# Agent attention and a max-out feed-forward layer in one kernel: the hand-written order of instructions replaced by another, and the last output tiles scaled by one engine instead of two

## The chip, the cores and the metric

The kernel runs on one core of a Trainium2 chip. The metric is the device time of one execution in microseconds (us), smaller being better. The times below are of three executions.

## The reference

Two layers run one after the other. The first is attention through 49 "agents" for each of 4 batches of 12544 rows of 128 numbers; the second is a feed-forward layer on all 50176 rows with three input matrices of 128 x 768, whose products are combined by a maximum.

```python
def sm(a, b):
    s = scale * (a @ b.transpose(0, 2, 1))
    s = s - s.max(-1, keepdims=True)
    e = np.exp(s)
    return e / (e.sum(-1, keepdims=True) + 1e-09)
a2k = sm(agents, k)
agent_v = a2k @ v
q2a = sm(q, agents)
x = (q2a @ agent_v)                       # rows of all batches, one after the other
h = np.maximum(np.maximum(x @ w1, x @ w2), x @ w3)
out = h @ w_out
```

## The kernel before

The kernel folds the two layers into each other. For a batch b it first goes over all keys and values: it computes the exponentials of agents times keys, their sums, and the values that they weight. That gives a 49-row matrix, the agent values. Their products with the feed-forward matrices (the differences w3 - w1 and w2 - w1, and w1 times w_out) are kept as a tile `G` of 49 rows, used for all queries of that batch. A query tile then needs only its exponentials `e`, two products with `G` (`u` and `v`), two maxima, and the product with `w_out`.

**Names.** Every step is a small function with a name, made in `graph()` and put out by the class `Emit`. `kl`, `vl` and `ql` are loads of keys, values and queries; `kc`, `vc` and `qc` are their casts to bf16; `kt`, `ke`, `ks`, `kx` are the turn of a key chunk, its copy out of PSUM, its scores and its exponentials; `to` and `kv` add the sums and the weighted values into one PSUM tile `acc`. `vd` is the part of a value cast that VectorE does. A chunk is nine tiles of 128 rows; the first batch has ten such chunks and two of four tiles (numbers 10 and 11). `wm.0` to `wm.9` are ten spare products with the identity, whose results nobody reads.

**The head.** Of the first batch everything has to be loaded before any query can be finished. When the last value chunk is in, the step `rc0` sums the columns of `acc` and takes the reciprocal (lines 434 and 436), and `nr0` scales the agent values (L439). `gpa`, `gpc`, `gpb`, `gpd` are the products with the differences (L450), `gva` to `gvd` their copies into `G` (L457 on ScalarE, L459 on VectorE). The differences themselves are `d31a`, `d31b`, `d32`, `d21a`, `d21b` on VectorE (L409); `cw1`, `tw1`, `ew1`, `pl`, `el` prepare w1 times w_out.

**The body.** There are 49 query blocks s of 1024 rows. Each has scores and exponentials (`sc`, `ex`), the sums and their reciprocals (`su` L556, `re` L561), six pairs of products `u.s.f` and `v.s.f` (L569) with a first maximum on ScalarE (`a`, L582), a second on VectorE (`x`, L585), and two output tiles of 128 x 512 with the products `li` and `p` (L606, L615) and the scaling `ov` on VectorE (L624). The chunks of the next batch's keys and values are worked off between the products of the blocks. The last block, number 48, has one output tile of four row tiles and two of two (`o.48.1`, `o.48.2`). The last of these lies in a two-bank PSUM buffer, one row tile in each bank: its first row tile is scaled by VectorE (`ov.48.2`), the other by ScalarE (`ow.48`, L631). The four parts of the block are stored one by one (`st.48.0` to `st.48.3`, L639), the last from ScalarE's queue.

**What sets the order.** Nothing is scheduled by a machine. A long text, `ORDER`, names all 2901 steps in the order in which they are issued; each engine works its own steps in that order. A number behind a slash is the buffer that the step's new tile takes from its class (`SLOTS`): there are 13 load buffers, 3 for bf16 keys, 4 for bf16 values, 3 two-bank PSUM buffers (`UV`) and 2 one-bank ones (`OM`). A step that reuses a buffer waits for the last reader of the tile before it. All loads, the turns by DMA and nearly all stores are issued by SyncE, also in that order.

Of the kernel before, what the change touches and what calls it, by code (L numbers as in the profile page):

```python
# [115 lines left out]
def graph(plan, em):  # L116
# [93 lines left out]
    for s in range(NQ):  # L210
# [61 lines left out]
class Emit:  # L272
# [315 lines left out]
    def out_chunks(self, s, o):  # L588

        if s < NQ - 1 or o == 0:  # L590
            return [(4 * o + i, i * C) for i in range(4)]
        return [(4, 0), (5, C)] if o == 1 else [(6, 0), (7, 512)]

    def out_linear(self, s, o):
        def fn():
            of = [p[0] for p in parts_of(s) for _ in range(p[4])]
            out, chunks = self.flat(f"o.{s}.{o}") if o == 2 else self.t[f"o.{s}.{o}"], self.out_chunks(s, o)
            if o == 2:
                for j, c in chunks:
                    jj, h = j // 2, j % 2  # L600
                    self.nc.tensor.matmul(out[:, c:c + C], self.t[f"e.{s}"][:, jj * P:(jj + 1) * P],
                                          self.t[f"G{of[jj]}"][:, C1O + h * C:C1O + (h + 1) * C], start=True, stop=False, skip_group_check=True)
                return
            for j, c in chunks[::2]:
                jj = j // 2
                self.nc.tensor.matmul(out[:, c:c + 2 * C], self.t[f"e.{s}"][:, jj * P:(jj + 1) * P],  # L606
                                      self.t[f"G{of[jj]}"][:, C1O:C1O + 2 * C], start=(c == 0), stop=False, skip_group_check=True)
        return fn

    def out_hidden(self, s, o, f):  # L610
        def fn():
            out = self.flat(f"o.{s}.{o}") if o == 2 else self.t[f"o.{s}.{o}"]
            for j, c in self.out_chunks(s, o):
                jj, h = j // 2, j % 2
                self.nc.tensor.matmul(out[:, c:c + C], self.t[f"r.{s}.{f}"][:, h, jj * P:(jj + 1) * P], self.wo_bf[:, f, :],  # L615
# [3 lines left out]
    def out_scale(self, s, o):  # L619
        def fn():  # L620
            chunks = self.out_chunks(s, o)
            j, n = chunks[0][0], 1 if o == 2 else len(chunks)
            out = self.flat(f"o.{s}.{o}") if o == 2 else self.t[f"o.{s}.{o}"]
            self.nc.vector.tensor_tensor(out=self.t[f"os.{s}"][:, j:j + n, :],  # L624
                                         in0=out[:, :n * C].rearrange("p (j c) -> p j c", c=C),
                                         in1=self.t[f"rc.{s}"][:, j:j + n].unsqueeze(2).to_broadcast([P, n, C]), op=ALU.mult)
        return fn

    def out_scale_last(self, s):
        def fn():  # L630
            self.nc.scalar.activation(self.t[f"os.{s}"][:, 7, :], self.flat(f"o.{s}.2")[:, 512:512 + C], AF.Copy,  # L631
                                      scale=self.t[f"rc.{s}"][:, 7:8])
        return fn
# [48 lines left out]
kl0.10/0 kc0.10/0 kl0.5/1 kl0.0/2 kc0.5/1 prep kc0.0/2 kt0.0/0 kt0.10/1 kt0.5/2 ke0.10/0 ke0.0/1 vl0.7/3 kl0.7/4 kl0.6/5 vc0.7/0  # L682
kc0.7/2 kc0.6/1 kt0.6/0 ke0.6/2 ks0.0/1 kt0.7/0 ke0.7/1 ks0.7/0 ke0.5/1 kx0.0/0 ks0.6/1 ks0.5/2 kl0.11/6 vl0.5/7 kl0.1/8 kc0.11/0
kx0.5/1 to0.0/0 kt0.11/2 ke0.11/1 vc0.5/1 kx0.6/2 ql.0/9 kl0.9/0 kc0.9/2 kt0.9/2 to0.5 kv0.5 kx0.7/3 to0.7 ks0.11/0 kx0.11/1
kl0.2/1 vl0.0/2 kc0.2/1 vc0.0/1 kv0.0 kv0.7 vl0.2/3 qc.0/0 vl0.11/4 qt.0/1 ke0.9/2 ks0.9/0 kx0.9/3 vc0.2/0 qe.0/0 vc0.11/1 vd0.11
ks0.10/2 vl0.10/10 kl0.8/6 kl0.4/5 vl0.9/11 to0.6 wm.1/1 kc0.1/0 kt0.1/1 kt0.2/0 ke0.1/0 to0.9 ke0.2/2 wm.0/1 ks0.2/0 vl0.6/12
sc.0/1 kc0.4/0 kt0.4/1 vc0.9/2 kv0.9 to0.11 kv0.11 kx0.10/0 to0.10 ex.0/0 kc0.8/1 kt0.8/2 ke0.4/2 ke0.8/1 kl0.3/0 vl0.8/7 kx0.2/3
# [5 lines left out]
pl/1 el u.0.4/1 a.0.4 sc.1/0 kc1.2/2 v.0.0/2 x.0.0/2 gl/1 gvl ex.1/1 v.0.3/0 x.0.3/3 v.0.4 x.0.4/4 qt.2/1 qe.2/0 u.1.5/2 a.1.5/0  # L693
li.0.0/0 p.0.0.0 u.0.2/1 a.0.2/2 vc1.0/0 v.1.5/0 x.1.5/5 u.1.2/2 a.1.2/1 vl1.2/2 p.0.0.4 p.0.0.5 v.0.2/1 x.0.2/6 u.1.3/0 a.1.3/0
sc.2/1 ex.2/2 p.0.0.3 p.0.0.1 v.1.3/2 x.1.3/7 u.1.4/1 a.1.4 u.1.1/0 a.1.1/2 p.0.0.2 ov.0.0/0 li.0.1/1 p.0.1.2 p.0.1.4 v.1.2/2
v.1.4 x.1.4/4 x.1.2/6 p.0.1.1 p.0.1.5 u.2.5/0 a.2.5/0 p.0.1.3 p.0.1.0 ov.0.1 u.2.4/1 a.2.4 v.1.1/2 x.1.1/2 ql.4/3 qc.3/1 qt.3/0
qe.3/0 u.1.0/0 a.1.0/1 li.1.0/1 v.2.4 x.2.4/3 v.1.0/2 x.1.0/1 p.1.0.2 p.1.0.3 kt1.0/2 p.1.0.1 ks1.0/0 su.1 v.2.5/0 x.2.5/0 kx1.0/3
# [205 lines left out]
```

## Time and profile before

| what | value |
|---|---|
| times of three executions | 446.63, 445.02, 448.14 us |
| median | 446.63 us |
| the profiled execution | 447.16 us |
| its span, first to last instruction | 445.4 us |
| so outside the span | 1.76 us |
| mean granted TensorE clock | 0.996 |
| TensorE, VectorE, ScalarE, GpSimd busy | 423.2, 390.5, 393.1, 169.5 us |

The profile is of one execution, and its times are microseconds from the start of the span. PE is TensorE's matmul stream and PEld its weight loads, DVE is VectorE, ACT is ScalarE, POOL is GpSimd, SP is SyncE. In the timeline a row gives the start, the duration, the engine, the line of the kernel, the operation, the tile written and the tiles read, and in brackets how long the engine had been idle and what ended that. PE rows join several matmuls, and their ends are modelled.

### The profile page before, as it was taken

The numbers are of one execution on the slowest core, as the hardware profiler recorded it, in microseconds if no ns is written. First come the engines' busy times: TensorE is split into PE (matmuls) and PEld (weight loads), VectorE is DVE, ScalarE is ACT, GpSimd is POOL, SyncE is SP. The second block draws the span as 40 slices with busy tenths as digits, with TensorE's granted clock in tenths as the row PEclk, the third lists the DMA queues.
The fourth block names the chain that finished last, engine by engine and source line by source line (L and its number), as shares of the span: only waits on it lengthen the run. The fifth ranks groups of instructions, "written<-read, shape, count | busy, mean of one in ns | idle before, by whom it ended". The sixth has DMA issues, their size and how long they took to land.

```text
span 445.4 us, 12837 instructions
## 1 busy us (share of the span) xinstructions
PE 423.2 (95%) x5247; PEld 270.6 (61%) x5247; DVE 390.5 (88%) x495; ACT 393.1 (88%) x462; POOL 169.5 (38%) x176
## 2 busy tenths in 40 slices
PE   2687999999999999999999999999999999999996
PEld 2464466666666666666666666665665655556676
DVE  2335898999999999999999899999999999999996
ACT  2258899999998999999999999999999999999983
POOL 3522645468537437380745435354402002000000
PEclk9999899999999999999999999999999999999999
DMA  8999999999999999999999999999997952562144
GB/s 322 410 411 349 349 297 233 296 411 313 274 415 308 237 385 352 328 202 360 415 410 202 247 331 307 284 295 308 250 252 220 232 164 71 120 198 64 49 168 166
DMA packets 99158, 122.50 MB, mean 275 GB/s; under 512 B 72536, under 2 KB 75292, under 8 KB 99100
## 3 DMA queue, kind: packets, MB, share of 16 engines
q1 hardware_dynamic: 98752, 121.46, 90.9%
q8 instruction: 41, 0.67, 0.6%
q10 hardware_dynamic: 347, 0.23, 0.2%
q14 instruction: 18, 0.14, 0.1%
HBM read 78.74 MB, written 25.69 MB: 234 GB/s over the span
## 4 chain that ended last, share of the span: by engine, by line
PE 86%; DMA 4%; ACT 4%; DVE 3%; issue 2%; SPq 0%; POOL 0%; DVEq 0%; ACTq 0%; POOLq 0%
PE UV L569 35%; PE OM L615 31%; PE OM L606 6%; PE OM L544 3%; PE OM L387 3%; DMA LD<-in_k_dram 2%; PE OM L534 2%; PE OM L370 2%; ACT AS L582 2%; DMA LD<-in_v_dram 2%; DVE R L585 2%; PE OM L556 1%; PE UV L353 1%; ACT VB L344 1%; DVE OS L624 1%
## 5 line engine op out<-in xcount | busy, mean ns | idle before, releaser
L585 DVE TENSOR_TENSOR R<-UV,AS 128x1024 bf16<-128x1024 f32 x245 | 293.0, 1218 | 17.4 <-PE UV L569 14.3
L582 ACT ACTIVATE AS<-UV 128x1024 bf16<-128x1024 f32 x245 | 246.2, 1025 | 18.0 <-PE UV L569 13.8
L569 PE MATMUL UV<-EQ,G 49*128 49x512 bf16 (+1 forms) x1248 | 183.1, 370 | 0.8 <-ACT AS L582 0.2
L615 PE MATMUL OM<-wo_bf,R 128*128 128x128 bf16 x2340 | 178.7, 220 | 0.0
L615 PEld LDWEIGHTS <-R 128*128 128x128 bf16 x2352 | 139.1, 98 | 42.1 <-issue 39.6
L569 PEld LDWEIGHTS <-G 49*128 49x128 bf16 x1248 | 60.9, 93 | 62.8 <-issue 22.6
L528 POOL CAST QB<-LD 128x1024 bf16<-128x1024 f32 x49 | 50.9, 1043 | 109.7 <-DMA LD<-in_q_dram 59.2
L624 DVE TENSOR_TENSOR OS<-OM,RC 128x512 f32<-128x512 f32 x98 | 66.9, 683 | 3.4 <-PE OM L615 2.3
L346 POOL CAST KB<-LD 128x1152 bf16<-128x1152 f32 (+2 forms) x45 | 50.0, 1118 | 35.6 <-DMA LD<-in_k_dram 24.7
L576 ACT ACTIVATE UV<-UV 128x1024 f32<-128x1024 f32 x49 | 49.8, 1017 | 2.7 <-PE UV L569 1.6
L579 ACT ACTIVATE R<-UV 128x1024 bf16<-128x1024 f32 x49 | 50.2, 1024 | 1.1 <-PE UV L569 0.4
L346 POOL CAST VB<-LD 128x1152 bf16<-128x1152 f32 (+1 forms) x33 | 37.2, 1137 | 34.2 <-DMA LD<-in_v_dram 22.6
L485 POOL TENSOR_TENSOR EA<-EA,EK 128x441 f32<-128x441 f32 x27 | 27.6, 1024 | 31.2 <-ACT EK L376 31.0
L606 PE MATMUL OM<-G,EQ 128*128 128x256 bf16 x195 | 37.8, 275 | 0.0
L550 ACT ACTIVATE EQ<-OM 128x512 bf16<-128x512 f32 x49 | 29.5, 603 | 1.4 <-PE OM L544 1.4
L358 DVE COPY KT<-UV 128x1152 bf16<-128x1152 bf16 (+1 forms) x12 | 8.3, 702 | 18.3 <-PE UV L353 17.7
L606 PEld LDWEIGHTS <-EQ 128*128 128x128 bf16 x195 | 12.3, 97 | 15.0 <-issue 14.7
L370 PEld LDWEIGHTS <-KT 128*128 128x128 bf16 x392 | 15.0, 100 | 8.5 <-DVE KT L358 4.1
L544 PE MATMUL OM<-QT,agT 128*64 128x512 bf16 (+1 forms) x104 | 19.9, 388 | 0.0
L387 PE MATMUL OM<-EK,VB 128*128 128x49 bf16 x392 | 17.6, 187 | 2.2 <-ACT VB L344 1.5
L376 ACT ACTIVATE EK<-OM 128x441 bf16<-128x441 f32 (+1 forms) x33 | 18.0, 544 | 1.1 <-PE OM L556 0.5
L387 PEld LDWEIGHTS <-VB 128*128 128x128 bf16 x392 | 14.4, 98 | 7.4 <-issue 4.0
(73 smaller groups left out, 191.4 us busy)
## 6 DMA issues: line engine op xcount, KB each, us to landing
LD<-in_q_dram SPq DMA_DIRECT2D x48, 512.0 KB, 7.4
out_dram<-OS SPq DMA_DIRECT2D x48, 512.0 KB, 5.3
LD<-in_k_dram SPq DMA_DIRECT2D x40, 576.0 KB, 9.6
LD<-in_v_dram SPq DMA_DIRECT2D x40, 576.0 KB, 8.8
LD<-in_k_dram SPq DMA_DIRECT2D x3, 512.0 KB, 6.9
LD<-in_v_dram SPq DMA_DIRECT2D x3, 512.0 KB, 7.4
LD<-in_moe_w_dram SPq DMA_DIRECT2D x6, 192.0 KB, 8.2
KT<-KB SPq DMA_TRANSPOSE x33, 5.7
```

The lines of the kernel that those rows point to most:

```text
L346: (self.nc.gpsimd if eng == POOL else self.nc.vector).tensor_copy(out=out, in_=src)
L387: self.nc.tensor.matmul(out, vb[:, j, :], e[:, j * A:(j + 1) * A], start=False, stop=True, skip_group_check=True)
L528: return lambda: self.nc.gpsimd.tensor_copy(out=self.t[f"qb.{s}"], in_=self.t[f"q.{s}"][:, :GT, :])
L544: self.nc.tensor.matmul(self.t[f"qs.{s}"][h * H:(h + 1) * H, jj * P:(jj + pairs) * P], self.agT[:, b, :], self.t[f"qT.{s}"][:, 2 * jj + h: ...
L569: self.nc.tensor.matmul(t[:, h, jj * P:(jj + pairs) * P], self.t[f"G{b}"][h * H:h * H + A, c + f * P:c + (f + 1) * P], self.t[f"e.{s}"][h ...
L576: return lambda: self.nc.scalar.activation(self.t[f"u.{s}.{f}"], self.t[f"u.{s}.{f}"], AF.Relu)
L579: return lambda: self.nc.scalar.activation(self.t[f"r.{s}.{f}"], self.t[f"u.{s}.{f}"], AF.Relu)
L582: return lambda: self.nc.scalar.activation(self.t[f"a.{s}.{f}"], self.t[f"u.{s}.{f}"], AF.Relu)
L585: return lambda: self.nc.vector.tensor_tensor(out=self.t[f"r.{s}.{f}"], in0=self.t[f"v.{s}.{f}"], in1=self.t[f"a.{s}.{f}"], op=ALU.max)
L606: self.nc.tensor.matmul(out[:, c:c + 2 * C], self.t[f"e.{s}"][:, jj * P:(jj + 1) * P], self.t[f"G{of[jj]}"][:, C1O:C1O + 2 * C], start=(c ...
L615: self.nc.tensor.matmul(out[:, c:c + C], self.t[f"r.{s}.{f}"][:, h, jj * P:(jj + 1) * P], self.wo_bf[:, f, :], start=False, stop=True, ski ...
L624: self.nc.vector.tensor_tensor(out=self.t[f"os.{s}"][:, j:j + n, :], in0=out[:, :n * C].rearrange("p (j c) -> p j c", c=C), in1=self.t[f"r ...
```

## The change

`ORDER` is replaced by another text. The same steps are in it, without `ow.48`. From the first line on the loads come in another sequence (the set of nineteen loads up to `vl0.9` is the same, and so is the sequence of the six value and key loads and the six weight loads behind it), the key chunks are turned in another order, the ten spare products stand elsewhere, and buffers are numbered anew. Between the blocks 1 and 31 steps of GpSimd and SyncE, single products `p` and the order of neighbouring `u`, `v`, `a`, `x` differ; from the second output tile of block 31 on the order of the steps is the same up to the buffers' numbers. In the last block both `o.48.1` and `o.48.2` now lie as 256 adjacent columns in one bank, `li.48.2` is one product of 256 columns where it was two of 128, and `ov.48.2` scales both row tiles on VectorE in one instruction; `ow.48` and its function are gone.

```diff
-            add(f"ov.{s}.{o}", DVE, em.out_scale(s, o), (0.19, 0.28) if o == 2 else (0.345, 0.45) if quarter else (0.634, 0.72),
+            add(f"ov.{s}.{o}", DVE, em.out_scale(s, o), (0.345, 0.45) if quarter else (0.634, 0.72),
                 after=[f"p.{s}.{o}.{f}" for f in range(NF)] + [f"re.{s}"],
...
-            if o == 2:
-                add(f"ow.{s}", ACT, em.out_scale_last(s), (0.28, 0.37), after=[f"p.{s}.{o}.{f}" for f in range(NF)] + [f"re.{s}"],
-                    use=[f"o.{s}.{o}", f"rc.{s}", f"os.{s}"])
...
     def out_chunks(self, s, o):
-        if s < NQ - 1 or o == 0:
-            return [(4 * o + i, i * C) for i in range(4)]
-        return [(4, 0), (5, C)] if o == 1 else [(6, 0), (7, 512)]
+        return range(4) if o == 0 else range(4, 8) if s < NQ - 1 else range(2 * o + 2, 2 * o + 4)

     def out_linear(self, s, o):
...
+            out, tiles = self.flat(f"o.{s}.{o}"), self.out_chunks(s, o)
+            for j in tiles[::2]:
+                c = (j - tiles[0]) * C
+                self.nc.tensor.matmul(out[:, c:c + 2 * C], self.t[f"e.{s}"][:, j // 2 * P:(j // 2 + 1) * P],
+                                      self.t[f"G{of[j // 2]}"][:, C1O:C1O + 2 * C], start=(c == 0), stop=False, skip_group_check=True)
...
-    def out_scale_last(self, s):
-        def fn():
-            self.nc.scalar.activation(self.t[f"os.{s}"][:, 7, :], self.flat(f"o.{s}.2")[:, 512:512 + C], AF.Copy,
-                                      scale=self.t[f"rc.{s}"][:, 7:8])
-        return fn
```

The order from the cast of value chunk 9 to the first products of block 0, before and after:

```diff
-vc0.9/2 kv0.9 to0.11 kv0.11 kx0.10/0 to0.10 ex.0/0 kc0.8/1 kt0.8/2 ke0.4/2 ke0.8/1 kl0.3/0 vl0.8/7 kx0.2/3
-to0.2 vc0.10/1 vc0.6/2 ks0.1/0 ks0.8/2 kv0.2 kx0.8/1 vl0.4/8 vl0.3/9 wm.5/1 kv0.6 wm.6/1 ks0.4/2 kx0.1/3 to0.1 vl0.1/1 lw3a/2
-lw1a/3 lw1b lw2a/11 lw3b lw2b kc0.3/1 kt0.3/0 ke0.3/2 wm.2/1 ql.1/0 qc.1/0 ks0.3/0 vd0.10 kv0.10 lwo/10 cwo vc0.8/2 ql.2/7 qc.2/1
-kx0.4/2 to0.4 vc0.4/0 wm.8/2 kx0.3/0 to0.3 ql.3/8 kl1.1/12 to0.8 kv0.4 wm.7/0 wm.4/2 vl1.0/6 kl1.0/5 kl1.2/4 vc0.3/1 kv0.3 kv0.8
-rc0/0 d31a vc0.1/0 kv0.1 nr0/0 cw1 su.0/1 re.0/0 wm.3/2 gpa/0 gva wm.9/2 d21a gpc/1 gvc u.0.1/0 a.0.1/0 d31b d32 gpb/2 tw1/1 d21b
-gpd/1 kc1.1/1 kc1.0/0 gvb u.0.5/2 a.0.5/1 gvd v.0.1/0 x.0.1/0 u.0.3/1 a.0.3/2 ew1 qt.1/0 qe.1/0 u.0.0/2 a.0.0/0 v.0.5/0 x.0.5/1
+to0.6 ke0.9/2 kt0.11/0 ke0.11/0 ks0.11/0 kx0.11/2 vc0.0/0 vd0.11 to0.11 kv0.11 ke0.1/0 ks0.1/2 kx0.1/2 kt0.4/0 kl0.3/7 vl0.8/8
+ke0.2/0 vl0.4/6 ks0.10/2 kv0.0 to0.1 vc0.9/0 ks0.9/1 kx0.9/0 kc0.8/2 ke0.4/1 kt0.8/0 vc0.6/1 vl0.3/10 sc.0/1 ke0.8/2 ks0.8/0
+wm.2/1 to0.9 kv0.5 kv0.9 vl0.1/2 vc0.10/2 ks0.2/1 kx0.2/0 kx0.8/1 lw3a/9 lw1a/3 kv0.6 lw1b lw2a/12 lw3b lw2b ex.0/0 ks0.4/1
+kc0.3/2 kt0.3/0 to0.8 ql.1/7 qc.1/0 lwo/0 cwo kx0.4/3 to0.4 to0.2 kv0.2 vc0.8/1 kx0.10/0 vc0.4/3 ke0.3/1 ks0.3/0 to0.10 kv0.8
+wm.9/2 wm.6/1 kx0.3/1 to0.3 wm.1/0 su.0/1 re.0/0 wm.7/1 ql.2/6 qc.2/1 vd0.10 kv0.4 wm.4/1 rc0/0 vc0.3/1 d31a wm.3/0 vl1.0/5 kv0.3
+kv0.10 vc0.1/0 kv0.1 cw1 wm.8/0 nr0/0 gpa/0 gva wm.5/1 kl1.0/2 d21a kc1.0/2 gpc/2 gvc kl1.1/10 u.0.1/0 a.0.1/0 d31b d32 gpb/1 d21b
+gpd/2 gvb u.0.5/1 a.0.5/1 gvd vc1.0/0 v.0.1/0 x.0.1/0 u.0.3/2 a.0.3/2 tw1/0 ew1 qt.1/1 qe.1/0 u.0.0/1 a.0.0/0 kl1.2/8 kc1.1/1
```

The last steps, before and after:

```diff
-ov.48.1 st.48.2 p.48.2.4 p.48.2.0 p.48.2.5 p.48.2.1 p.48.2.3 ow.48 ov.48.2 st.48.3
+ov.48.1 st.48.2 p.48.2.4 p.48.2.0 p.48.2.5 p.48.2.1 p.48.2.3 ov.48.2 st.48.3
```

More of the change, by code (lines that the diff above doesn't have):

```diff
@@ L681 @@
 ORDER = """
[L682 to L685, printed above, removed]
@@ L694 @@
[L694 to L697, printed above, removed]
@@ L870 @@
-p.48.0.0 x.48.4/12 p.48.0.4 x.48.3/7 p.48.0.3 li.48.1/1 ov.48.0/2 li.48.2/0 p.48.1.5 st.48.1 st.48.0 p.48.1.2 p.48.2.2 p.48.1.1
-p.48.1.0 p.48.1.4 p.48.1.3 ov.48.1 st.48.2 p.48.2.4 p.48.2.0 p.48.2.5 p.48.2.1 p.48.2.3 ow.48 ov.48.2 st.48.3
+kl0.10/0 kc0.10/0 kl0.5/1 kl0.0/2 kc0.5/1 prep kt0.10/0 kt0.5/1 kc0.0/0 kt0.0/2 ke0.0/0 ke0.10/1 kl0.7/3 vl0.7/4 vc0.7/0 kl0.6/5
+kc0.6/0 kt0.6/0 ke0.6/2 kl0.1/6 kc0.7/1 kt0.7/2 ks0.0/0 ke0.7/0 ks0.7/2 kx0.0/0 ke0.5/0 ks0.5/1 to0.0/0 ks0.6/0 kx0.5/1 ql.0/7
+kl0.9/8 vl0.11/9 wm.0/1 vc0.11/1 kx0.7/2 to0.7 kx0.6/3 kl0.11/0 kc0.11/1 qc.0/0 qt.0/1 kc0.9/0 kt0.9/0 to0.5 vl0.2/1 kl0.2/2
```

382 lines of the change are left out of this document (187 added, 195 removed).

## The prediction

> **What bounds the kernel now.** I read the page first, for the shape of the whole.
>
> ```profile
> PE 423.2 (95%) x5247; PEld 270.6 (61%) x5247; DVE 390.5 (88%) x495; ACT 393.1 (88%) x462; POOL 169.5 (38%) x176
> ...
> PE   2687999999999999999999999999999999999996
> ...
> DMA  8999999999999999999999999999997952562144
> ```
>
> There is a head of some four slices (11 us each) in which TensorE is not full and the DMA engines are, and then a body in which TensorE never rests. Then I cut the span into windows; the columns are the window, its length, the busy time of PE, PEld, DVE, ACT and POOL, the granted clock, the DMA share and GB/s.
>
> ```profile
> 28.00:30.00 2.00, 1.94 (x20) 1.92 (x19) 0.76 (x1) 1.31 (x3) 0.68 (x1) 1.00 1.03 415
> ...
> 37.40:40.80 3.40, 2.56 (x46) 1.63 (x47) 0.56 (x2) 3.40 (x5) 0.00 (x0) 1.00 0.87 304
> 40.80:44.20 3.40, 2.21 (x23) 0.95 (x23) 3.37 (x10) 2.25 (x4) 1.17 (x1) 0.99 1.01 347
> 44.20:47.60 3.40, 3.40 (x22) 1.60 (x21) 2.14 (x4) 1.53 (x3) 1.90 (x2) 0.51 1.00 385
> ...
> 48.00:335.00 287.00, 286.38 (x3642) 182.33 (x3641) 271.12 (x341) 272.65 (x323) 142.94 (x145) 1.00 1.07 309
> 335.00:442.00 107.00, 106.68 (x1243) 66.94 (x1239) 101.44 (x112) 97.15 (x108) 9.25 (x9) 1.00 0.50 144
> ```
>
> From 48 to 442 us TensorE lacks 0.94 us of 394, with VectorE and ScalarE at some 94%. So the body moves as a whole: what the head gives or loses comes out at the end, as long as the pace of the body stays. The head ends when the agent values are scaled (L439), and just behind it the clock is at 0.51 for 3.4 us. Four places can move: the end of the loads' work, the short chain behind it, the clock, and the last stores.
>
> **The loads and ScalarE.** The timeline of ScalarE from the last wait for a load:
>
> ```profile
> 29.74 1.16 ACT L344 ACTIVATE VB<-LD 128x1152 bf16<-128x1152 f32 x1 [0.69 <-DMA LD<-in_v_dram]
> 30.81 0.32 ACT L376 ACTIVATE EK<-UV 128x196 bf16<-128x196 f32 x1
> 31.79 0.60 ACT L550 ACTIVATE EQ<-OM 128x512 bf16<-128x512 f32 x1 [0.66 <-PE OM L544]
> ...
> 38.03 0.55 ACT L376 ACTIVATE EK<-UV 128x441 bf16<-128x441 f32 x1
> 38.44 2.23 ACT L344 ACTIVATE VB<-LD 128x1152 bf16<-128x1152 f32 x2
> ```
>
> The same casts by form (shortest, middle and longest ns):
>
> ```profile
> L344 ACT ACTIVATE VB<-LD x12: 406/1159/1183, 9.2 to 39.5; 128x1152 bf16<-128x1152 f32 x10, 128x256 bf16<-128x256 f32 x2
> ```
>
> At 29.74 it starts the cast `vc0.9`, whose load it waited for, so it had no backlog then. From there it does thirteen more steps up to the end of `vc0.1` at 38.44 + 2.23 = 40.67, with one wait of 0.66 us, for `sc.0` on TensorE. In the new order the loads ahead of `vl0.9` are the same nineteen, so it should land at the same time; behind `vc0.9` there are again one small and five full value casts, `ex.0`, five full exponentials and a small one, only in another sequence (`kx0.9` instead of `kx0.1`). So `vc0.1` can end at 40.67 - 0.66 = 40.0 at the earliest. What can be late instead is `kx0.2`: TensorE's queue ahead of it holds `kt0.8`, `sc.0`, `ks0.8`, a spare product, `to0.9`, `kv0.5`, `kv0.9`, `ks0.2`, which is 9 transposes, 36 small products and 3 long ones.
>
> ```profile
> 24.90 0.93 PE L387 MATMUL OM<-EK,VB 128*128 128x49 bf16 x18 [1.54 <-ACT VB L344]
> 27.05 0.54 PE L381 MATMUL OM<-EK,ones_bf 128*128 128x441 bf16 x1
> 28.08 2.08 PE L353 MATMUL UV<-ident,KB 128*128 128x128 bf16 x18
> 32.69 0.66 PE L353 MATMUL UV<-ident,KB 128*128 128x128 bf16 x9
> 33.27 0.35 PE L381 MATMUL OM<-EK,ones_bf 128*128 128x441 bf16 x1
> 39.68 0.64 PE L387 MATMUL OM<-EK,VB 128*128 128x49 bf16 x18
> ```
>
> The upper three rows are slow and the lower three fast, though the clock column says 1.00 for 28 to 30 us: the durations show that TensorE only came to speed near 31 us. By the slow rows the queue takes 9 x 2.08/18 + 36 x 0.93/18 + 3 x 0.54 = 4.5 us, by the fast ones 0.66 + 36 x 0.64/18 + 3 x 0.35 = 3.0. It starts with the cast of key chunk 8, whose load is the one ahead of `vl0.9`. That is 0.59 MB at 415 GB/s, or 1.4 us earlier, near 28.3; with a cast on GpSimd (1.17 in the row of `qc.1` further down) TensorE can start at 29.5. `kx0.2` may then start between 32.5 and 34.0, while ScalarE comes to it at 29.74 + 1.16 + 0.55 + 1.16 + 0.41 = 33.0 (`vc0.9`, `kx0.9`, `vc0.6`, and the small `vc0.10`, of whose form the line L344 has 0.406). So the new wait is between 0 and 1.0 us. I take 0.36, because the clock rose near 31 us, a third into this queue: -0.66 + 0.36 = **-0.3 us**, bounds -0.66 and +0.4.
>
> **From the last cast to the agent values.** The chain goes through VectorE:
>
> ```profile
> 40.36 0.62 DVE L434 TENSOR_REDUCE KR<-OM 128x49 f32<-128x441 f32 x1 [2.84 <-PE OM L387]
> 41.01 0.46 DVE L436 RECIPROCAL KR<-KR 128x49 f32<-128x49 f32 x1
> 41.39 0.49 DVE L409 TENSOR_TENSOR wall<-LD,LD 128x384 bf16<-128x384 f32 x1
> 41.80 0.20 DVE L439 TENSOR_TENSOR avT<-OM,KR 128x49 bf16<-128x49 f32 x1
> 41.91 0.20 DVE L561 RECIPROCAL RC<-OM 128x8 f32<-128x8 f32 x1
> 42.03 2.42 DVE L409 TENSOR_TENSOR wall<-LD,LD 128x384 bf16<-128x384 f32 x5
> ```
>
> ```profile
> 41.03 0.39 PE L387 MATMUL OM<-EK,VB 128*128 128x49 bf16 x9 [0.71 <-DVE KR L434]
> ```
>
> Today `rc0` stands behind `kv0.3` and `kv0.8`, and `kv0.1` waits 0.71 us until the reduction has read `acc`; then `d31a` stands ahead of the scaling. From the end of `vc0.1` to the scaling are 41.80 - 40.67 = 1.13 us. In the new order `rc0` follows `kv0.4`, which hangs on `vc0.4`, a cast that ended before `kx0.3`; so reduction, reciprocal and `d31a` (40.36 to 41.88, 1.5 us) run while ScalarE does the last two casts (2.23 us). `rc0` itself starts some 1.3 us after `kx0.3`: `to0.3`, `su.0`, `kv0.4` and two spares stand ahead of it, each of some 0.3. `d31a` then ends 2.8 us after `kx0.3`, the last values at 2.23 + 0.39 + 0.05 = 2.7. So the scaling starts some 0.65 to 0.75 us after `vc0.1`, instead of 1.13: **-0.4 us**, bounds -0.55 and 0, the latter if `rc0` is held up. Behind the scaling `re.0` (41.91 to 42.03, 0.12) no longer stands ahead of `d21a`: **-0.1 us**.
>
> **The differences beside GpSimd.** `gpb` at 44.03 waits for `d31b` and `d32`, three pieces of 128 columns.
>
> ```profile
> L409 DVE TENSOR_TENSOR wall<-LD,LD x6: 283/499/1123, 41.4 to 43.9; 128x384 bf16<-128x384 f32 x3, 128x128 bf16<-128x128 f32 x3
> ```
>
> ```profile
> 42.67 1.17 POOL L528 CAST QB<-LD 128x1024 bf16<-128x1024 f32 x1 [8.04 <-DMA LD<-in_q_dram]
> 44.03 0.50 PE L450 MATMUL UV<-wall,avT 128*64 128x384 bf16 x2 [0.65 <-DVE wall L409]
> 44.47 0.82 PE L421 MATMUL OM<-ident,w_bf 128*128 128x128 bf16 x6
> 45.22 0.53 PE L450 MATMUL UV<-wall,avT 128*64 128x384 bf16 x2
> 45.68 1.46 PE L569 MATMUL UV<-EQ,G 49*128 49x512 bf16 x6
> ```
>
> One piece took 1.123 us where another took 0.283, while GpSimd cast `qc.1` from 42.67 to 43.84. The Trainium skill, GPSIMD Engine Reference, section 1 (Specifications), says that GpSimd's SBUF interfaces are shared with VectorE and that instructions with two SBUF inputs contend; the row agrees with it. If all comes some 0.8 us earlier and `qc.1` does not (its load stands behind the same bytes), the pieces are through before the cast and 1.123 - 0.283 = 0.84 us goes; if `qc.1` comes earlier too, nothing. I take **-0.3 us**, bounds -0.84 and 0.
>
> **The clock and `tw1`.** Between 44.2 and 47.6 us TensorE ran at 0.51, which costs up to 3.4 x 0.49 = 1.67 us of its work. The window before that has 2.21 us of TensorE in 3.4. In the new order six spare products stand between `kx0.3` and `gpc` where there were four (0.35 each), and the wait of 0.71 goes, so the stretch is denser; `tw1` (0.82) leaves the place between `gpb` and `gpd`, so `u.0.5` can follow `gvb`, at up to 0.5 us less. What the clock gives is not won whole, since u, a, v, x pass through three engines. How busy the window must be the trace doesn't say; 2.56 in 3.4 was enough before it. Half a chance of about 0.8 is **-0.4 us**, bounds -1.67 and +1.7 (a second slow window). The Trainium skill, TensorE: Matmul & The Clock Gate, Part 1, says that the clock falls after an idle window of about 3.4 us; here it fell without a gap of even 1 us, so the measurement decides against that wording, and by that rule neither kernel would lose here.
>
> **The tail.**
>
> ```profile
> 441.30 0.72 PE L615 MATMUL UV<-wo_bf,R 128*128 128x128 bf16 x10
> 441.50 0.42 DVE L624 TENSOR_TENSOR OS<-OM,RC 128x256 f32<-128x256 f32 x1 [0.31 <-PE OM L615]
> 442.06 0.37 ACT L631 ACTIVATE OS<-UV,RC 128x128 f32<-128x128 f32 x1 [2.44 <-PE UV L615]
> 442.46 0.29 DVE L624 TENSOR_TENSOR OS<-UV,RC 128x128 f32<-128x128 f32 x1 [0.53 <-ACT OS L631]
> 442.79 0.38 ACTq L639 DMA_DIRECT2D out_dram<-OS  x1
> ```
>
> The two halves are not scaled at once: VectorE waits for ScalarE. From 442.06 to 442.75 are 0.69 us; one piece of 256 columns has a row of its own, 0.42. So **-0.27 us**, firm within 0.1. The product `li.48.2` in one piece stands on a queue that still waits for others: 0.
>
> **The body.** The steps moved between blocks 1 and 31 are the same steps, and no duration changes. Their cover is the 0.94 us slack of TensorE and the waits of VectorE for products:
>
> ```profile
> DVE R L585 <- PE UV L569: 10.9, 32, 0.8
> ```
>
> These are 10.9 us in 32 waits from 44 to 335 us. I take 0, bounds -1 and, if the cover is gone, one more such amount.
>
> **The sum:** -0.3 - 0.4 - 0.1 - 0.3 - 0.4 - 0.27 = -1.77 us. Against the profiled execution, 447.16 us, that is 445.39; that execution is 0.53 above the median of the three runs, so for a median run I say 446.63 - 1.77 = **444.9 us**.
>
> **The rivals.**
>
> *The wait moves.* TensorE is still slow at the queue ahead of `kx0.2`, so ScalarE waits 1.0 us and `vc0.1` ends at 41.0. With +0.4, -0.4, -0.1, the cold window as before and the tail -0.27, the time is 446.63 - 0.37 = 446.3. For it speaks the slow rate up to 31 us; against it that the new order has TensorE dense from the cast of chunk 4 on.
>
> *A second slow clock window* (slower): the value chunks come in 1.15 us steps and TensorE has 0.4 us of work for each, so the clock can fall before the products and again stay low behind them. The head's -0.3 - 0.4 - 0.1 and the tail's -0.27 stay, and +1.67 comes: 447.2. Against it: 2.56 of 3.4 us held the clock.
>
> *The body loses its pace* (slower): with the products in another order between blocks 1 and 31, VectorE waits longer for v. It has 94% to do, so it cannot catch up. From a total of 10.9 + 1.8 = 12.7 us of such waits on, the change is a loss; at three quarters more, +8.2, the time is 446.63 - 1.77 + 8.2 = 453.1. For it: three engines are nearly full, and nothing in the trace bounds it. Against it: in each block u, a, v, x keep nearly their sequence.
>
> *The head gives all.* The wait for `sc.0` goes whole (0.66), the chain gives 0.55 and 0.12, the contention 0.84, the clock stays up (1.67), `u.0.5` follows `gvb` (0.5), the tail 0.27: -4.6, 442.0 us.
>
> **How the numbers follow.** The forecast, 443.4 to 446 with 444.9 in it, has 0.45; the moved wait 0.19, the second slow window 0.13, the body 0.13, the full gain 0.10. The range of 442.8 to 449.0 us takes in the forecast, the first two rivals and the spread of the runs (445.02 to 448.14), and leaves out most of the last two. About 1% (4.5 us) is what a measurement of this kernel can tell from no change. Faster by more than that is under 442.2, half of the full gain: 0.05. Slower by more is over 451.1, nearly all of the body's rival: 0.12. The rest, 0.83, is within.
>
> **What would show it.** In the new profile: the scaling L439 starts at 40.6 to 41.3 instead of 41.80; L434 runs before the last value cast ends, and the last L387 no longer waits for it; no wait for L544 on ScalarE, or another one for L370 of at most 1.0; the longest L409 piece is under 0.5; the clock from 43 to 48 us is above 0.51; the last L624 is one of 128x256 with 0.42, followed by the store. DVE's waits for UV between 44 and 335 us stay near 10.9. The forecast is wrong if L439 is later than 41.8, if the clock is low for over 4 us, or if TensorE's busy time from 48 to 335 us falls under 285.

## The result, and the profile after

| | before | after |
|---|---|---|
| median of 12 runs, us | 446.19 (443.56 to 450.42) | 443.01 (442.27 to 444.06) |
| ratio after / before | | 0.9927 [0.9901, 0.9953] |
| profiled execution, us | 447.16 (span 445.4) | 442.68 (span 440.9) |

The new kernel is 3.2 us faster at the median. Its runs lie within 1.8 us, those of the old one within 6.9. The forecast was 444.9 in a range of 442.8 to 449.0; the measured time lies 0.2 us above the low end of that range and below the 443.4 to 446 that had the largest chance. The ratios here and below leave out executions more than 1.5% above the fastest of their kernel, so they are not the quotients of the medians beside them. The code lost three lines above the places of the head, so L439 is now L436, L409 is L406, L450 is L447, L569 is L566 and L585 is L582; further down it lost more, and L624 is now L611.

First the windows of the new profile, with the same edges as before (window, length, busy time of PE, PEld, DVE, ACT and POOL, granted clock, DMA share, GB/s):

```profile
37.40:40.80 3.40, 2.99 (x42) 1.39 (x37) 3.18 (x10) 2.91 (x6) 0.00 (x0) 1.00 1.08 370
40.80:44.20 3.40, 3.02 (x29) 1.50 (x30) 3.09 (x6) 3.00 (x5) 1.87 (x2) 1.00 1.05 395
44.20:47.60 3.40, 3.29 (x29) 1.68 (x30) 3.40 (x4) 3.40 (x6) 1.37 (x2) 1.00 1.02 406
48.00:335.00 287.00, 286.30 (x3653) 182.53 (x3650) 271.06 (x340) 271.42 (x320) 143.96 (x147) 1.00 1.10 312
```

The clock stays at 1.00 and the body keeps its pace: 286.30 of 287 us against 286.38. So the time came from the head and the tail. Rows of the new timeline of ScalarE up to its last value cast:

```profile
18.28 0.54 ACT L373 ACTIVATE EK<-UV 128x441 bf16<-128x441 f32 x1 [2.27 <-PE UV L367]
...
25.69 0.33 ACT L373 ACTIVATE EK<-UV 128x196 bf16<-128x196 f32 x1 [2.18 <-PE UV L367]
...
28.35 1.17 ACT L341 ACTIVATE VB<-LD 128x1152 bf16<-128x1152 f32 x1 [0.84 <-DMA LD<-in_v_dram]
...
31.27 0.42 ACT L341 ACTIVATE VB<-LD 128x256 bf16<-128x256 f32 x1 [0.28 <-PE OM L384]
...
36.30 2.23 ACT L341 ACTIVATE VB<-LD 128x1152 bf16<-128x1152 f32 x2
```

`vc0.1` ends at 36.30 + 2.23 = 38.53 instead of 40.67. VectorE and TensorE behind it:

```profile
38.66 0.49 DVE L406 TENSOR_TENSOR wall<-LD,LD 128x384 bf16<-128x384 f32 x1
39.07 0.20 DVE L436 TENSOR_TENSOR avT<-OM,KR 128x49 bf16<-128x49 f32 x1
39.34 1.78 DVE L406 TENSOR_TENSOR wall<-LD,LD 128x384 bf16<-128x384 f32 x5
40.70 0.82 PE L447 MATMUL UV<-wall,avT 128*64 128x384 bf16 x4
41.72 0.85 PE L566 MATMUL UV<-EQ,G 49*128 49x512 bf16 x6 [0.19 <-DVE G L456]
42.43 1.23 DVE L582 TENSOR_TENSOR R<-UV,AS 128x1024 bf16<-128x1024 f32 x1 [0.31 <-PE UV L566]
```

The row of before for that last one, `x.0.1`, the first result of block 0:

```profile
46.83 1.23 DVE L585 TENSOR_TENSOR R<-UV,AS 128x1024 bf16<-128x1024 f32 x1 [0.48 <-PE UV L569]
```

Read as a chain, the 4.40 us between the two profiles at `x.0.1` are:

| step | before | after | difference |
|---|---|---|---|
| end of `vc0.1` | 40.67 | 38.53 | -2.14 |
| `vc0.1` to the scaling `nr0` | 1.13 | 0.54 | -0.59 |
| `nr0` to `gpb` | 2.23 | 1.63 | -0.60 |
| `gpb` to `u.0.5` | 1.65 | 1.02 | -0.63 |
| `u.0.5` to `x.0.1` | 1.15 | 0.71 | -0.44 |

The last two lie nearly whole in the window whose clock was 0.51 before (from 44.2). At the end:

```profile
437.08 0.72 PE L604 MATMUL UV<-wo_bf,R 128*128 128x128 bf16 x10
437.84 0.42 DVE L611 TENSOR_TENSOR OS<-UV,RC 128x256 f32<-128x256 f32 x1
438.29 0.39 ACTq L620 DMA_DIRECT2D out_dram<-OS  x1
```

From the end of the last product to the issue of the store are 438.29 - 437.80 = 0.49 us; before they were 442.79 - 442.02 = 0.77. The span ends 3.1 us after the last product (440.9 - 437.80), and ended 3.4 after it before (445.4 - 442.02), so the end comes earlier by as much.

A caution on reading one pair of profiles: the old kernel's executions differ among themselves. Each run has the mean clock that was granted, and one window of 3.4 us at half clock lowers it by about 0.004 (3.4 x 0.5 of some 443 us). So a change's own effect is read here from the runs at full clock, and the clock is counted apart. Full clock means a mean of 0.999 or more, and a window at half clock is called cold. Beside the experiments the old kernel ran at full clock in 17 of 35, 21 of 35 and 11 of 17 runs, with means of 445.65, 445.26 and 445.92; its other runs had, by that count, one to four cold windows and took 447.2 to 452.5. The new kernel was at full clock in 11 of 12 runs, with a mean of 443.19, and its twelfth, with one cold window, took 443.06. For the old kernel's twelve runs in the table the record has no clocks.

### The profile page after: what moved, and what is told of

It reads as the page before. It is cut to its first block, busy times and chain, and to the rows that moved or that the text cites. A ratio compares the mean times of both kernels' runs of the same rounds, so it can differ in the third digit from the quotient of the medians.

```text
span 440.9 us, 12824 instructions
## 1 busy us (share of the span) xinstructions
PE 421.0 (95%) x5246; PEld 268.6 (61%) x5246; DVE 390.6 (89%) x495; ACT 392.4 (89%) x461; POOL 169.3 (38%) x176
## 4 chain that ended last, share of the span: by engine, by line
PE 74%; DMA 15%; ACT 3%; POOL 3%; SPq 2%; DVE 1%; issue 1%; DVEq 0%; ACTq 0%; POOLq 0%
PE UV L566 31%; PE OM L604 28%; DMA LD<-in_k_dram 8%; PE OM L595 5%; PE OM L541 3%; DMA LD<-in_q_dram 2%; ACT AS L579 2%; DMA LD<-in_moe_w_dram 2%; DMA LD<-in_v_dram 2%; PE OM L384 2%; PE OM L531 2%; PE OM L367 2%; DMA KT<-KB 1%; SPq L333 1%; POOL KB L343 1%
## 5 line engine op out<-in xcount | busy, mean ns | idle before, releaser
L582 DVE TENSOR_TENSOR R<-UV,AS 128x1024 bf16<-128x1024 f32 x245 | 293.1, 1218 | 17.2 <-PE UV L566 13.2
L566 PE MATMUL UV<-EQ,G 49*128 49x512 bf16 (+1 forms) x1248 | 182.6, 369 | 1.0 <-DVE G L456 0.2
L566 PEld LDWEIGHTS <-G 49*128 49x128 bf16 x1248 | 60.4, 93 | 63.6 <-issue 23.3
L611 DVE TENSOR_TENSOR OS<-OM,RC 128x512 f32<-128x512 f32 x98 | 66.8, 681 | 3.0 <-PE OM L604 2.0
L341 ACT ACTIVATE VB<-LD 128x1152 bf16<-128x1152 f32 (+1 forms) x12 | 12.3, 1040 | 9.9 <-DMA LD<-in_v_dram 9.6
```

Of the source, the lines that this page charges most:

```text
L566: self.nc.tensor.matmul(t[:, h, jj * P:(jj + pairs) * P], self.t[f"G{b}"][h * H:h * H + A, c + f * P:c + (f + 1) * P], self.t[f"e.{s}"][h ...
L582: return lambda: self.nc.vector.tensor_tensor(out=self.t[f"r.{s}.{f}"], in0=self.t[f"v.{s}.{f}"], in1=self.t[f"a.{s}.{f}"], op=ALU.max)
```

## The experiments

The theory was that two things were won, and that neither is the pace of the body: some 2 us in the head by the time of the agent values, and the clock behind it by a denser TensorE. The rivals were that the order of the body, the loads' sequence alone, or the tail carry the gain. In diffs of the order the buffers' numbers are left out. Each kernel ran 12 times (the ninth 6 times), in three groups on three chips, each with the old kernel beside it: experiments 1, 2, 3 and 5, then 4, 6, 7 and 8, then 9 and 10. The new kernel itself ran in none of them, so what is set against its 443.19 is set against another group.

**1. The tail alone** (old order).

```diff
-p.48.2.4 p.48.2.0 p.48.2.5 p.48.2.1 p.48.2.3 ow.48 ov.48.2 st.48.3
+p.48.2.4 p.48.2.0 p.48.2.5 p.48.2.1 p.48.2.3 ov.48.2 st.48.3
```

> The old order with the new last block (o.48.1 and o.48.2 in one piece each on VectorE, no step ow.48). Tail theory: the end falls by 0.27 us, the last 256-column scaling starts where ScalarE's started and takes 0.42; in the time 446.2 - 0.3 = 445.9, not to be told from no change by the clock on the wall, so the trace decides: from the end of the last product to the issue of the last store 0.49 us instead of 0.77. Rival, that the last stores finish together whatever the scaling does: the issue is earlier, the end of the span after the last product is not.

Measured: 448.65 against 447.82, ratio 1.0004 [0.9961, 1.0048]. The rows of the end are as in the new kernel:

```profile
444.15 0.72 PE L604 MATMUL UV<-wo_bf,R 128*128 128x128 bf16 x10
445.36 0.39 ACTq L620 DMA_DIRECT2D out_dram<-OS  x1
```

They give 0.49 us again, and the span ends 3.1 us after the last product as in the new kernel, so the rival falls. The 0.28 is shown by the rows and is far below what the times resolve: seven of the twelve runs had cold windows, and the five at full clock have a mean of 444.86. In this profile the clock stayed low for some three windows in a row (0.76, 0.50, 0.50 and 0.74 in the four from 44.2 to 57.8 us), behind a window in which TensorE had 1.81 us of work:

```profile
40.80:44.20 3.40, 1.81 (x19) 0.59 (x15) 3.40 (x9) 2.05 (x4) 2.23 (x3) 1.00 1.04 393
44.20:47.60 3.40, 3.29 (x26) 1.77 (x28) 3.18 (x6) 1.96 (x2) 1.92 (x2) 0.76 1.02 412
47.60:51.00 3.40, 3.40 (x18) 1.03 (x14) 1.88 (x4) 2.31 (x4) 1.69 (x2) 0.50 1.03 410
```

**2. The new head with the old body, and 3. the old head with the new body** (both with the new tail). The orders are cut at the first product of block 0's output, `p.0.0.0`.

```diff
 e2_head: new order up to p.0.0.0, ql.3 next, then the old order
 e3_body: old order up to p.0.0.0, then the new order
```

> The new head up to the first product p.0.0.0, then the old order of the body, and the new tail. Head theory (all but 0.27 us of the gain arises before block 0's first products): 443.0 to 443.4 us, as the whole change. Body theory (half of the gain or more comes from the order between blocks 1 and 31): 444.6 us or more.

> The old head up to p.0.0.0, then the new order of the body, and the new tail. Head theory: 446.2 - 0.3 = 445.9 us, with the spread of several us of the kernel before. Body theory: 444.3 us or less.

Measured: the head alone 449.54, ratio 1.0034 [1.0000, 1.0069]; the body alone 447.69, ratio 1.0020 [0.9975, 1.0065], with 446.00 at full clock against 445.65, so the body's order by itself gives nothing. The head alone has its values early (`nr0` at 39.45) and still ends late; ten of its twelve runs also lost a window of clock, and the two at full clock have 447.23. So its head theory (443.0 to 443.4) did not come true. The cut was at fault in part: `ql.3` came to stand first in SyncE's queue, which then issued nothing from 40.2 to 51.74, as the queue's timeline shows:

```profile
38.92 1.28 SPq L333 DMA_DIRECT2D LD<-in_k_dram  x3
51.74 0.33 SPq L521 DMA_DIRECT2D LD<-in_q_dram  x1
```

**4. A cleaner cut**: the new order up to `ql.3` in block 1, where both orders have done the same steps, then the old order, with the new tail.

```diff
 e8_join: ... x.1.1 (new order up to here) ql.3
-kt1.0 vl1.1 qc.3 qt.3
+ql.4 qc.3 qt.3 (old order from here on; kt1.0 and vl1.1 come 14 and 22 steps behind ql.3)
```

> The new head up to ql.3 in block 1, where both orders have issued the same set of steps, then the old order of the body, and the new tail: a cleaner join than the run before, in which SyncE stood at ql.3 until 51.7 us. Head theory: 443.0 to 443.4 us. Body theory (the order between blocks 1 and 31 gives half of the gain or more): 444.5 us or more, with TensorE's busy time between 51 and 335 us lower than in the changed kernel.

Measured: 446.12, ratio 0.9999 [0.9966, 1.0031], 445.35 at full clock. `nr0` stands at 38.98, as early as in the new kernel, but the gain is given back in the body. The windows of this kernel, and the same two of the new one:

```profile
54.40:60.00 5.60, 4.21 (x57) 2.50 (x56) 3.72 (x5) 4.13 (x5) 2.63 (x3) 1.00 1.34 298
150.00:250.00 100.00, 98.95 (x1269) 63.63 (x1269) 94.01 (x119) 94.12 (x111) 48.07 (x49) 1.00 1.09 316
```

```profile
54.40:60.00 5.60, 5.60 (x80) 3.65 (x79) 5.13 (x6) 5.57 (x8) 2.24 (x3) 1.00 1.26 209
150.00:250.00 100.00, 99.77 (x1270) 63.83 (x1268) 94.92 (x118) 94.42 (x112) 47.41 (x49) 1.00 1.10 324
```

TensorE loses 1.39 and 0.82 us there. In the first window it stands for want of ScalarE:

```profile
58.58 0.39 PE L566 MATMUL UV<-EQ,G 49*128 49x512 bf16 x2 [1.39 <-ACT R L576]
```

GpSimd waits 3.29 us in that window for the load `vl1.1`, which the old order issues behind the transpose of `kt1.0`. That wait alone doesn't explain the stand: in the old kernel GpSimd waits 3.3 us for a value load between 50 and 62 us too, and TensorE does not stand there. Of the 2.2 us between 445.35 and 443.19, some 0.3 lie outside the span (2.05 to 2.24 us in these runs, 1.75 to 1.89 in the new kernel's), for a reason that isn't known.

So the body's order wins nothing with the old head, and with the new head the old body loses what was won. That the new body's order is what keeps the gain is argued, not shown: both joins of a new head to the old body may have a cost of their own.

**5. The chain alone**: in the old order, the reduction ahead of the last two casts.

```diff
-kl1.1 to0.8 kv0.4 wm.7 ... vc0.3 kv0.3 kv0.8 rc0 d31a vc0.1 kv0.1 nr0 cw1 su.0 re.0 wm.3
+kl1.1 to0.8 su.0 re.0 kv0.4 wm.7 ... rc0 d31a vc0.3 kv0.3 kv0.8 vc0.1 kv0.1 nr0 cw1 wm.3
```

> The old order with four steps moved: su.0 and re.0 behind to0.8, rc0 and d31a ahead of vc0.3. Chain theory: from the end of the last value cast to the scaling of the agent values 0.5 to 0.6 us instead of 1.13, and some 0.1 behind it; in the time 0.6 to 0.7 less (445.5). Rival, that the head is set by the clock and by the loads: the chain shortens in the trace but the time does not move by more than 0.2, or the clock's window behind it eats it up.

Measured: 444.98 against 447.82, ratio 0.9936 [0.9902, 0.9971]; full clock in 11 of 12 runs, with a mean of 444.82 against 445.65. The rows:

```profile
38.37 2.30 ACT L344 ACTIVATE VB<-LD 128x1152 bf16<-128x1152 f32 x2
41.17 0.21 DVE L439 TENSOR_TENSOR avT<-OM,KR 128x49 bf16<-128x49 f32 x1 [0.18 <-PE OM L387]
40.80:44.20 3.40, 2.96 (x27) 1.22 (x27) 3.22 (x8) 2.50 (x4) 1.98 (x2) 1.00 1.07 397
```

From `vc0.1` (38.37 + 2.30) to the scaling are 0.50 us, where 1.11 to 1.13 are with the reduction behind the cast. With the reduction out of its way TensorE has 2.96 us of work in the window from 40.8 where it had 2.21 or 1.81, and the clock held. Four steps moved give 0.8 us at full clock and most of what the clock took, and the chain theory holds. By the medians that is nearly as much as the whole change (2.8 of 3.2 us); at full clock 1.6 us are left between 444.82 and the new kernel's 443.19.

**6. Without the late spare products**: the new order without six of them.

```diff
-to0.3 wm.1 su.0 re.0 wm.7 ... kv0.4 wm.4 rc0 vc0.3 d31a wm.3 ... cw1 wm.8 nr0 gpa gva wm.5
+to0.3 su.0 re.0 ... kv0.4 rc0 vc0.3 d31a ... cw1 nr0 gpa gva
```

> The new order without the six spare products between kx0.3 and gpc (wm.1, wm.7, wm.4, wm.3, wm.8, wm.5). Clock theory (the new kernel is faster in the median because TensorE is busy enough in the windows of 3.4 us around the agent values, and its clock doesn't fall): without them the granted clock falls in most executions, by one to three windows, and the median rises from 443.0 to 445 or more, with a spread like that of the kernel before. Rival, that the steps' order makes the stretch dense enough: no execution below 0.996 of mean clock, 443.0 us within 0.4.

**7. More spare products in the old order**: five added.

```diff
+kv0.8 wm.10 rc0 ... kv0.1 wm.11 nr0 cw1 su.0 re.0 wm.3 wm.12 gpa ... u.0.1 wm.13 wm.14
```

> The old order with five more spare products in the gaps between kv0.8 and gpb (fifteen in all). Clock theory: the mean clock is 0.999 or 1.0 in nearly all executions and the median is the mean of the old kernel's executions at full clock, 445.6, instead of 447.8 over all; the scaling of the agent values does not move (41.3 to 41.8). Rival, that the clock falls for what TensorE does before 40 us: the spread stays, 446 to 452 in half of the executions.

Measured without: 446.03 against 446.49, ratio 1.0000 [0.9968, 1.0031], and not one of 12 runs at full clock. Measured with more: 446.60, ratio 1.0002 [0.9969, 1.0036], and all 12 at full clock. Both clock theories hold for the clock; the seventh had the time 1.0 us too low, and its `nr0` comes at 40.96, ahead of the 41.3 to 41.8 expected. The window ahead of the fall, without the products:

```profile
37.40:40.80 3.40, 1.89 (x40) 1.28 (x36) 1.77 (x5) 3.40 (x5) 0.00 (x0) 1.00 0.97 346
40.80:44.20 3.40, 2.52 (x19) 0.70 (x17) 2.62 (x8) 2.42 (x4) 1.04 (x1) 0.70 1.04 369
```

So spare products between the last casts and the first products hold the clock in either order. In this profile of the sixth the clock was low once more, ahead of the place where products were taken out (0.69 and 0.81 in the windows from 27.2 to 34.0 us); that fall isn't theirs. Most of its runs have a mean clock of 0.991 or 0.992, that is two cold windows, as many as the later fall makes up. They are not free: with five more, the old order's runs at full clock take 446.60 against 445.26. The five products stand in the chain, and the differences met GpSimd's cast (3.08 us for five pieces); how the 1.3 us divide between these stays open.

**8. The new order with the old sequence of the first 19 loads, and 9. the reverse** (the diff is that of the eighth).

```diff
-the new order's loads: kl0.7 vl0.7 kl0.6 kl0.1 ql.0 kl0.9 vl0.11 kl0.11 vl0.2 kl0.2 vl0.5 ...
+the old order's:        vl0.7 kl0.7 kl0.6 kl0.11 vl0.5 kl0.1 ql.0 kl0.9 kl0.2 vl0.0 vl0.2 vl0.11 ...
```

> The new order with the first nineteen loads in the old sequence. Order theory (the agent values come 2.3 us earlier because ScalarE no longer stands behind TensorE's products, the loads ahead of vl0.9 being the same): the scaling still starts near 39.3 and the median is 443.0 to 443.5. Loads theory (the sequence of the loads is what brings the value chunks earlier): the scaling starts at 41 or later, the median is 444.5 or more.

> The old order of steps with the sequence of the first 19 loads of the new one. If the loads' sequence by itself brings the earlier agent values (vl0.9's part lands 1.4 us earlier, vc0.9 starts at 28.35 instead of 29.74), nr0 comes 1.5 to 2.5 us earlier than the 41.2 to 41.8 of the old heads, at 39.0 to 40.2, and the time at full clock falls by 1.3 to 2.0 us below the 445.3 to 445.7 of the old kernel. If sequence and order belong together, as the opposite pairing suggests (new order with the old loads: nr0 at 44.08), ScalarE and VectorE then wait for pieces of q and k that land later than their casts stand: nr0 at 41 to 44, time at full clock 445.5 to 448.

Measured: 449.15, ratio 1.0057 [1.0024, 1.0090], and 451.88 against 446.36, ratio 1.0102 [1.0040, 1.0164]. `nr0` comes at 44.08 and 43.57, later than in either whole kernel. ScalarE then waits in both for loads that come out of their turn:

```profile
23.51 0.42 ACT L341 ACTIVATE VB<-LD 128x256 bf16<-128x256 f32 x1 [3.88 <-DMA LD<-in_v_dram]
```

```profile
21.93 1.16 ACT L344 ACTIVATE VB<-LD 128x1152 bf16<-128x1152 f32 x1 [1.95 <-DMA LD<-in_v_dram]
```

So the order theory of the eighth fell, and in the ninth the second of the two came true for `nr0` (its one run at full clock took 448.18). Loads and steps belong together; neither half carries the gain. Each step kept its buffer in these two, so part of what they lose can be waits for buffers; that isn't separated.

**10. Towards a faster version**: the new order with the last two value casts split between ScalarE (five tiles) and VectorE (four).

```diff
-m = n if n == KT else 2
+m = 2 if n < KT else 5 if g in (3, 1) else n
-kx0.3 to0.3 ... vd0.10 kv0.4 wm.4 rc0 vc0.3 d31a wm.3 ... kv0.10 vc0.1 kv0.1 cw1
+kx0.3 vc0.3 vc0.1 to0.3 vd0.3 ... vd0.10 vd0.1 kv0.4 wm.4 rc0 d31a wm.3 ... kv0.10 kv0.1 (cw1 behind gvc)
```

> The new order with the last value casts of ScalarE split: of nine tiles each of vc0.3 and vc0.1, five on ScalarE and four on VectorE, and the first weight cast of w moved behind the agents' values. If the last ScalarE cast (vc0.1 ends at 38.53, nr0 starts 0.54 later) is what bounds the agents' values, nr0 comes 0.5 to 1.0 us earlier (38.1 to 38.6) and the time at full clock is 442.2 to 442.7. If the landing of the feed-forward weights (difference pieces from 38.66 on, ScalarE's wait of 0.37 for them at 38.90) is the next bound, nr0 comes earlier by as much, but the first gp moves by at most 0.4 from its 40.70 and the time stays within 442.8 to 443.3.

Measured: 443.90 against 446.36, ratio 0.9939 [0.9913, 0.9965]; at full clock 443.78 against 445.92, that is -2.14. Set against 443.19 and the 445.3 to 445.9 of before, it is no better than the new kernel. Both theories fell: `nr0` came later, at 40.05. The last half cast waited for its load, and the reduction stood behind VectorE's half:

```profile
38.24 0.74 ACT L341 ACTIVATE VB<-LD 128x640 bf16<-128x640 f32 x1 [0.35 <-DMA LD<-in_v_dram]
```

In this execution the loads were late as a whole. The first issue of the weights on SyncE, in the new kernel and in this one:

```profile
26.89 7.43 SPq L399 DMA_DIRECT2D LD<-in_moe_w_dram  x6
```

```profile
28.16 7.43 SPq L399 DMA_DIRECT2D LD<-in_moe_w_dram  x6
```

The weights' first issue came 1.27 us later, and the issue of `ql.0` near 4 us had taken 1.67 us instead of 0.47. With 1.27 added, the new kernel's `nr0` would stand at 40.34, so by this estimate the split is worth some 0.3, and here the landing of the last value chunk was the next bound.

## Why the prediction was right, and where its sizes were off

**The direction and the range held**; the sum did not: -1.77 us forecast, -3.18 between the medians. The time is nearer to the rival in which the head gives all (442.0, with a chance of 0.10) than to the forecast. Term by term:

**ScalarE and the loads: the term that failed in size** (-0.3 forecast, bounds -0.66 and +0.4). I began at 29.74, where the profile shows a wait for a load, concluded that ScalarE "had no backlog then", and counted only the waits behind it; of these I passed over one, 0.30 us at 32.68. The wait for the load hid longer ones ahead of it. The rows of the old profile from 16 us on in which ScalarE waits for TensorE, besides the 0.66 for `sc.0`:

```profile
19.27 0.54 ACT L376 ACTIVATE EK<-UV 128x441 bf16<-128x441 f32 x1 [3.86 <-PE UV L370]
23.46 0.33 ACT L376 ACTIVATE EK<-UV 128x196 bf16<-128x196 f32 x1 [1.74 <-PE UV L370]
27.16 0.54 ACT L376 ACTIVATE EK<-UV 128x441 bf16<-128x441 f32 x1 [2.31 <-PE UV L370]
32.68 0.54 ACT L376 ACTIVATE EK<-UV 128x441 bf16<-128x441 f32 x1 [0.30 <-PE OM L387]
```

These are 8.87 us with the 0.66. In the new profile they are 2.27, 2.18 and 0.28, that is 4.73; of the 4.14 saved, waits for loads take back 1.45 (2.14 against 0.69). The last wait ahead of `vc0.9` was for `ks0.9`: ScalarE stood 2.31 us for its scores. In the profile I read, the load was late as well, so the wait looked like the load's. In experiments 1 and 3, with the same old head, the weights' first issue is at 27.12 and 27.29 instead of 28.35, ScalarE does not wait for `vl0.9` at all, and `vc0.1` still ends at 40.23 and 40.42. This stretch of the timeline of experiment 1 shows it:

```profile
27.04 0.54 ACT L373 ACTIVATE EK<-UV 128x441 bf16<-128x441 f32 x1 [2.31 <-PE UV L367]
27.47 2.51 ACT L341 ACTIVATE VB<-LD 128x1152 bf16<-128x1152 f32 x3
```

So in the old head ScalarE is late behind TensorE, not behind the transfer. The new order has ScalarE busy for more of the same stretch, from 16 to 39 us, before and after:

```profile
16.00:39.00 23.00, 17.70 (x241) 13.04 (x240) 7.58 (x12) 13.96 (x22) 7.75 (x7) 1.00 1.02 400
```

```profile
16.00:39.00 23.00, 18.00 (x280) 13.20 (x280) 8.55 (x16) 15.65 (x25) 8.38 (x8) 1.00 1.03 405
```

1.69 us more of its work is done by 39 us. Among the profiles whose loads are about equally early (the weights' first issue at 26.89 to 27.29), `vc0.1` ends at 38.45 to 38.89 with the new head (the new kernel, experiments 2 and 4) and at 39.84 to 40.67 with the old one (experiments 1, 3, 5 and 7). That is 1.7 us in the mean; the rest of the 2.14 belongs to the one execution.

The prediction also carried the slow products, up to 31 us, over to the new order. There TensorE is at speed some 6 us earlier. The same sum of 441 columns in the new profile:

```profile
21.74 0.57 PE L378 MATMUL OM<-EK,ones_bf 128*128 128x441 bf16 x1
24.22 0.35 PE L378 MATMUL OM<-EK,ones_bf 128*128 128x441 bf16 x1
```

The first fast row is at 21.7 to 24.0 us in the five profiles with the new head and its loads, and at 28.0 to 31.0 in the five with the old head and its loads, while the clock column says 1.00 in both. So the slow queue that I feared ahead of `kx0.2` was not there, and that a wait of 0.28 came where I had put 0.36 is luck: it is for a value product. What late speed costs shows within the old order. Where the 18 transposes near 28 us take 1.18 and 1.19 us (experiments 3 and 7), `vc0.1` ends 11.85 and 11.86 us after their start; where they take 1.58 and 1.81 (1 and 5), 12.27 and 12.38. How much of the 1.7 us is the earlier speed and how much the order's shorter waits wasn't tried, nor which steps bring the speed forward.

**The chain** (-0.4; bounds -0.55 and 0): the mechanism was as described, `nr0` 0.54 us behind `vc0.1`, just past the bound at -0.59. Experiment 5 gives 0.50 by this alone. The further -0.1 for `re.0` did not come in this pair: from the scaling to the next differences are 0.27 us, and 0.23 before; in experiments 2 and 6 they are 0.11 and 0.12.

**The differences beside GpSimd** (-0.3; bounds -0.84 and 0): the five pieces took 1.78 instead of 2.42, and the cast of `qc.1` starts at 41.74, behind them. With the old head the price depends on when that cast comes: the pieces took 3.04 in experiment 1 and 1.58 in experiment 3, whose casts are these:

```profile
41.59 1.39 POOL L525 CAST QB<-LD 128x1024 bf16<-128x1024 f32 x1 [7.42 <-DMA LD<-in_q_dram]
```

```profile
43.17 1.07 POOL L525 CAST QB<-LD 128x1024 bf16<-128x1024 f32 x1 [8.80 <-DMA LD<-in_q_dram]
```

In experiment 3 the differences were all but through by then (43.35). So -0.64 in the pair, and up to -1.3 (3.04 against 1.78) where cast and pieces meet.

**The clock** (-0.4; bounds -1.67 and +1.7): the direction was right and so was the reason given, a denser stretch (experiments 5 and 6); "half a chance" was too little, and the price of 0.8 was too small: the last two steps of the chain, which `tw1` touches as well, are 1.07 us shorter. Against the runs at full clock, the old kernel's mean of all runs is 2.4, 1.8 and 1.4 us longer in the three groups, the new one's 0. Experiments 6 and 7 show that the spare products decide it, and experiment 5 that the order of the reduction does too. The rival of a second slow window is real in the old kernel, which has up to four, and did not come in the new one.

**The tail** (-0.27): -0.28. **The body** (0): 286.30 against 286.38, and VectorE's waits are as before:

```profile
DVE R L582 <- PE UV L566: 10.0, 27, 0.7
```

That no duration changes was a good reason for no gain, but not for no loss: in experiment 4 the old sequence behind the new head gives back 2.2 us, whether by its order or by the join. I had it down as the rival in which the new order loses pace; where pace was lost, it was with the old one.

Together, at full clock the agent values come some 2.1 us earlier (39.07, 39.45 and 38.98 with the new head against 41.34, 41.54 and 40.96 in experiments 1, 3 and 7), the tail gives 0.28, and 443.19 against 445.3 to 445.9, from other groups of runs, is 2.1 to 2.7. The clock gives the rest of the 3.2.

## What to carry to other kernels

A wait for a load at the head of a stretch doesn't show that the engine was ahead: look at what it waited for just before, and compare the busy time of the whole stretch. In a kernel whose body has no slack, a late head shows at the end (4.40 us at `x.0.1` and 0.28 in the tail, of 4.48 between the two profiled executions), and experiments 2 and 4 warn that a new head can lose its gain where it is joined to a body made for another. Where the clock can fall, take the distribution of the runs as part of what the kernel does: six products that nobody needs, placed where TensorE would thin out, decide here between medians of 443.0 and 446.0, in different groups of runs. Five more, which stand in the chain, hold the clock too, but the runs at full clock are 1.3 us longer.

## What the hardware showed beyond that

In the old profile the clock fell with no gap above 0.71 us ahead of it. By windows of 3.4 us with the edges used here, 1.81, 1.89 and 2.21 us of TensorE's work were followed by a clock of 0.76 and 0.50, of 0.70, and of 0.51. But the busy time of such a window doesn't decide by itself: in experiment 10, with TensorE at speed, 1.96 us from 23.8 to 27.2 were followed by 1.00, while in experiment 9 the clock fell behind 2.37.

```profile
40.80:44.20 3.40, 2.37 (x47) 1.54 (x45) 2.04 (x6) 2.38 (x3) 1.96 (x2) 1.00 0.98 353
44.20:47.60 3.40, 2.33 (x15) 1.13 (x15) 3.02 (x6) 1.90 (x3) 1.47 (x3) 0.67 1.02 409
```

Other edges give other sums, and no run here shows which stretch counts. Why the same program kept its clock in 49 of 87 runs and lost it in 38 was not tried. The table of the Trainium skill, TensorE: Matmul & The Clock Gate, Part 1, that puts the slow state after an idle window of about 3.4 us doesn't describe this: here the window was more than half busy.

VectorE's differences are slower beside GpSimd's cast: a piece of 128 columns went from 0.28 to 1.12 us. The cast itself took 1.39 instead of 1.04 us in experiment 1, but 1.04 in experiment 7, where the five pieces took 3.08.
